# Two crossbar transposes put side by side, a gate before three loads, and one permute moved from GpSimd to VectorE

## The chip, the cores and the metric

The kernel runs on one NeuronCore of a Trainium2 chip. The metric is the time of one execution on the device in microseconds. Beside it there is a profile of one execution: the time of every instruction on TensorE (PE, with its weight loads as PEld), VectorE (DVE), ScalarE (ACT), GpSimd (POOL) and of the DMA issues of SyncE (SP), and of the DMA packets.

## The reference

Attention in two steps through 32 packed tokens, and behind it a feed-forward layer with the activation h·cos(h):

```python
def sm_attn(qq, kk, vv):
    s = scale * np.matmul(qq, kk.transpose(0, 1, 3, 2))
    s = s - np.max(s, axis=-1, keepdims=True)
    a = np.exp(s)
    a = a / (np.sum(a, axis=-1, keepdims=True) + 1e-09)
    return np.matmul(a, vv)
p_packed = sm_attn(p, k, v)              # p: (8, 8, 32, 64), k and v: (8, 8, 576, 64)
attn = sm_attn(q, p_packed, p_packed)    # q: (8, 8, 576, 64)
x = attn.transpose(0, 2, 1, 3).reshape(8 * 576, 512)
h = x @ w_in                             # (512, 2048)
out = (h * np.cos(h)) @ w_out            # (2048, 512)
```

All inputs and the output are float32; the kernel works in bfloat16 with float32 accumulation.

## The kernel before

The work goes through the eight batch elements, b = 0 to 7, one after the other. For each b the kernel loads q, k and v (`load`, L82: a DMA issued by GpSimd that also casts to bfloat16). k and q are needed with the head dimension on the partitions. For b = 0 and 1 and for k2 this is done by transposes on TensorE and copies (`pe_T`, L95); for q2, k3 and all later ones by a DMA transpose that SP issues (`xbar`, L91). v is needed in another order of its free dimension; `permute_v` (L86) copies it within SBUF, on GpSimd except for b = 0, which VectorE does.

`s1(b)` computes the scores of p against k and their exponentials on ScalarE, `a1_pe`, `a1_one` or `a1_xbar` transposes them, and `recips(b)` (L148) takes the reciprocals of the sums and multiplies them by the scale (the two small VectorE operations at L151 and L152). `pp(b)` multiplies by v and leaves the packed result, transposed, in `ppT`. `s2(b)` computes the scores of q against it, `sums2` and `normalise` their normalisation. Because the second attention's values are the same 32 packed rows for each head, `ppw(b, n)` multiplies them by w_in first (the tile `PPW`, in four pieces n of 512 columns), and `h_mm(b, fc)` (L248) multiplies PPW by the normalised weights `a2n` for one of 16 chunks fc of the hidden dimension. ScalarE takes the cosine of the result, VectorE multiplies it by h into `gT` (L263), and GpSimd copies a corner of gT into `joint` twice in each slot (L267). `out_gen` (L301) is the product with w_out, cut into small steps.

The order is written out by hand (`tc.manual_schedule()`); each engine executes its instructions in that order, and only semaphores between the engines delay them. The sixteen `h_mm` of one b are a slot (`slot`, L420). Between them stand steps of the previous b's output (`fill(n)`, n matmuls each), and hooks: a hook `(fc, f)` calls f behind `h_mm(s, fc)` and before the fills that follow it. Slot 0 is written out at L404. PSUM holds three buffers for `psA` (scores, `h_mm`, `pp`, transposes) and two banks for `ot` (output, and whatever asks for `bank()`).

p is loaded in three pieces into `p_raw`: rows for b = 0 and rows for b = 1 by SP at the start, the others by GpSimd at L387. `dup_p` (L340) casts them into `p_bf` twice, and `pack_p` (L112) transposes them on TensorE into `P2`, which `s1` reads.

Loads are issued by GpSimd in the order of the code, each one behind what stands before it on GpSimd. Where loads are to start only after a crossbar has finished, a *gate* is put before them: a copy of one element of the crossbar's result by GpSimd (`G.tensor_copy(out=gate, in_=xT["k", ...])`, L496 and L522). The buffers for q and v in bfloat16 are single (`bufs=1`), those for k double, `vp` has two, and `osb`, from which SP stores the output, has four.

`warm(n)` issues n matmuls on zeros that nothing reads.

Of the kernel before, what the change touches and what calls it, by code (L numbers as in the profile page):

```python
# [9 lines left out]
BF16 = mybir.dt.bfloat16  # L10
# [5 lines left out]
def kernel(  # L16
# [10 lines left out]
    nc = tc.nc  # L27
    B, H, S, D = q.shape
# [26 lines left out]
    V, ACT, G = nc.vector, nc.scalar, nc.gpsimd  # L55
# [5 lines left out]
    gate = const.tile([1, 1], BF16, name="gate")  # L61
    P2 = const.tile([128, B, H, NP], BF16, name="P2")
    p_raw = const.tile([128, 2 * B, D], FP32, name="p_raw")
# [4 lines left out]
    p_rows = p.rearrange("b h n d -> (b h n) d").rearrange("(g r) d -> r g d", r=128)  # L68
    srcs = {"k": k, "q": q, "v": v}
    bf, vp, xT, a1T, sums1, r1, rs1 = {}, {}, {}, {}, {}, {}, {}  # L70
    a2u, lns, a2n, PPW = {}, {}, {}, {}

    def copy(eng, out, in_):
        if eng is ACT:
            ACT.copy(out=out, in_=in_)  # L75
        else:
            eng.tensor_copy(out=out, in_=in_)  # L77

    def psa(dt=FP32):
        return A.tile([128, 2, 512 if dt == FP32 else 1024], dt, name="psA", tag="A")  # L80

    def load(n, b):  # L82
        bf[n, b] = bf_pool.tile([TP, H, C * D], BF16, name=n + "bf", tag=n + "bf", bufs=2 if n == "k" else 1)
        G.dma_start(out=bf[n, b], in_=srcs[n][b].rearrange("h (p c) d -> p h (c d)", c=C))  # L84

    def permute_v(b, eng=G):  # L86
        vp[b] = vp_pool.tile([TP, C, H * D], BF16, name="vp", tag="vp")
        copy(eng, vp[b].rearrange("p c (h d) -> p c h d", h=H),
             bf["v", b].rearrange("p h (c d) -> p c h d", c=C))

    def xbar(n, b):  # L91
        t = xT[n, b] = att_pool.tile([128, H * 3, TP], BF16, name=n + "T", tag=n + "T", bufs=2 if n == "k" else 1)
        nc.sync.dma_start_transpose(out=t, in_=bf[n, b].rearrange("p h x -> p (h x)"))

    def pe_T(n, b, engs=(V, V, V), groups=(0, 1, 2), own=False):  # L95
        if 0 in groups:
            xT[n, b] = att_pool.tile([128, H * 3, TP], BF16, name=n + "T", tag=n + "T", bufs=2 if n == "k" else 1)
        t = xT[n, b]
        flat = bf[n, b].rearrange("p h x -> p (h x)")
        for i in groups:  # L100
            ps = bank(BF16) if own else psa(BF16)[:, 0, :]
            for j in range(8):
                o = 8 * i + j
                nc.tensor.transpose(ps[:, j * TP:(j + 1) * TP], flat[:, o * 128:(o + 1) * 128],  # L104
                                    ident[0:TP, 0:TP])
            copy(engs[i], t[:, 8 * i:8 * i + 8].rearrange("p a x -> p (a x)"),
                 ps[:, 0:8 * TP])

    def bank(dt=FP32):
        return O.tile([128, 512 if dt == FP32 else 1024], dt, name="ot", tag="ot")  # L110

    def pack_p(b0, b1, flat=None):  # L112
        ng = 2 * (b1 - b0)
        if flat is None:
            flat = psa(BF16).rearrange("p a x -> p (a x)")
        for g in range(ng):
            nc.tensor.transpose(flat[:, g * 128:(g + 1) * 128],
                                p_bf[:, 2 * b0 + g].rearrange("p t d -> p (t d)"), ident)
        V.tensor_copy(out=P2[:, b0:b1].rearrange("p b h n -> p (b h n)"), in_=flat[:, 0:ng * 128])
# [14 lines left out]
    def s1(b, later=False):  # L134
        ps = scores(P2[:, b], xT["k", b])
        sm = sums1[b] = small.tile([128, 2], FP32, name="sums1")

        def exps():
            for y in range(2):
                ACT.activation(  # L140
                    out=a1[b % 2][:, y, :, 0:TP].rearrange("p (e m) x -> p e m x", e=2),
                    in_=ps[y][:, :, 0:HS].rearrange("p e (m x) -> p e m x", m=3),
                    func=AF.Exp, scale=scale, accum_out=sm[:, y:y + 1])
        if later:
            return exps
        exps()
# [22 lines left out]
    def a1_one(b):  # L169
        t = a1T[b] = att_pool.tile([128, 2, C, 128], BF16, name="a1T", tag="a1T")  # L170
        ps = psa(BF16)
        for y in range(2):
            for c in range(C):
                nc.tensor.transpose(ps[0:TP, y, c * 128:(c + 1) * 128], a1[b % 2][:, y, c, 0:TP], ident)
        for y in range(2):
            copy(V, t[0:TP, y].rearrange("p c x -> p (c x)"), ps[0:TP, y, 0:C * 128])

    def pp(b, own=False, engs=(V, ACT)):
        ps = bank() if own else psa()[:, 0, :]
        for hp in range(4):  # L180
            for j in range(C):
                c = 2 * (j % 3) + j // 3
                nc.tensor.matmul(ps[:, hp * 64:(hp + 1) * 64], vp[b][:, c, hp * 128:(hp + 1) * 128],  # L183
                                 a1T[b][0:TP, :, j, 32 * hp:32 * hp + 32], start=(j == 0), stop=(j == C - 1))
        pv = ps[:, 0:256].rearrange("p (a y x) -> p a y x", a=4, y=2)
        t = ppT[b % 2].rearrange("p (a y) x -> p a y x", y=2)
        for y in range(2):
            r = slice(64 * y, 64 * y + 64)
            copy(engs[0], t[r, :, y, :], pv[r, :, y, :])
        for y in range(2):  # L190
            r = slice(64 * y, 64 * y + 64)
            z = slice(64 - 64 * y, 128 - 64 * y)
            copy(engs[1], t[z, :, y, :], pv[r, :, y, :])
# [27 lines left out]
    def s2(b):  # L221
        a2u[b] = att_pool.tile([128, 2, S], BF16, name="a2u", tag="a2u")
        ps = scores(ppT[b % 2], xT["q", b])
        for y in range(2):
            ACT.activation(out=a2u[b][:, y].rearrange("p (e x) -> p e x", e=2),  # L225
                           in_=ps[y][:, :, 0:HS], func=AF.Exp, scale=rs1[b][:, y:y + 1])
# [109 lines left out]
    def load_w_out(n):  # L336
        G.dma_start(out=w_out_bf[:, n * 4:(n + 1) * 4, :],
                    in_=moe_w_out.rearrange("(a p) n -> p a n", p=128)[:, n * 4:(n + 1) * 4, :])

    def dup_p(a, b, eng):  # L340
        for t in range(2):
            eng.tensor_copy(out=p_bf[:, a:b, t, :], in_=p_raw[:, a:b, :])

    def warm(n):
        wps = bank()
        for _ in range(n):
            nc.tensor.matmul(wps, wz[:, 0:128], wz, start=True, stop=True)  # L347

    for a in (0, 2):
        nc.sync.dma_start(out=p_raw[:, a:a + 2, :], in_=p_rows[:, a:a + 2, :])  # L350
    load("k", 0)
    load("v", 0)
    make_identity(nc, ident)
# [15 lines left out]
    pack_p(0, 1)  # L369
    warm(9)  # L370
    pe_T("k", 0, (V, ACT, V))
    s1(0)
    dup_p(2, 4, V)
    pack_p(1, 2, bank(BF16))
    permute_v(0, V)
    load("v", 1)
    load_w_in(3)
# [7 lines left out]
    for n in range(4):  # L385
        load_w_out(n)
    G.dma_start(out=p_raw[:, 4:, :], in_=p_rows[:, 4:, :])  # L387
    s2(0)
    warm(3)
    sums2(0, 0)  # L390
    sums2(0, 1)
    pe_T("k", 1, (V, V, V))
# [2 lines left out]
    cut_ppw, rest_ppw = ppw(0, 0, V, own=True, later=True, cuts=((0, 256), (256, 512)))  # L395
    normalise(0)
    s1_mm()
    cut_ppw()
    a1_one(1)
    rest_ppw()  # L400
    load("k", 2)
    permute_v(1)
    load("v", 2)
# [16 lines left out]
    def slot(s, hooks, keep=0, heavy={}):  # L420
        left = filler[1] - keep
        out_eng[:] = (ACT,) if s > 1 else (V, ACT)
        weight = [1 + heavy.get(fc, 0) for fc in range(NFC)]
        for fc in range(NFC):
            h_mm(s, fc)()
            quota = (left * sum(weight[:fc + 1])) // sum(weight) - (left + keep - filler[1])
            first = quota
            while hooks and hooks[0][0] == fc:
                if first == quota and fc in heavy:
                    first = quota // 2  # L430
                    fill(first)
                hooks.pop(0)[1]()
            fill(quota - first if first != quota else quota)

    def pw2(b, n=0, eng=None):
        ppw(b, n, eng)
        ppw(b, n + 1, eng)

    def tk(n, b, i):
        return lambda: pe_T(n, b, (V, V, V), (i,))  # L440

    ACT.preload_act_table_set(EXP_SET)
    fill(4)
    s2(1)
# [4 lines left out]
    fill(5)  # L449
    sums2(1, 0)  # L450
    sums2(1, 1)
    xbar("q", 2)
    permute_v(2)
    load("v", 3)
    permute_v(3)
    load("q", 3)
    ppw(1, 1, V)
    normalise(1)
    ACT.preload_act_table_set(SIN_SET)
    fill(14)  # L460
    slot(1, [(3, lambda: pw2(1, 2, (ACT, V))), (5, tk("k", 2, 0)), (6, tk("k", 2, 1)),
             (7, tk("k", 2, 2)), (8, lambda: load("k", 4)), (9, lambda: pack_p(2, 5)),
             (11, lambda: pack_p(5, B)), (12, lambda: xbar("k", 3))], 4, {3: 3})

    ACT.preload_act_table_set(EXP_SET)
    out_eng[:] = V,
# [30 lines left out]
    for n, b in (("v", 4), ("q", 4), ("k", 5)):  # L497
        load(n, b)
    fill(5)
    slot(2, [(7, lambda: pp(3, engs=(ACT, ACT))), (11, lambda: pw2(3))], 5, {11: 3})  # L500

    for s in range(3, B):
        nxt = s + 1 < B
# [66 lines left out]
```

## Time and profile before

| what | value |
|---|---|
| time, median of 5 runs | 253.81 us |
| the five runs | 254.0, 253.81, 249.42, 254.47, 253.64 us |
| the profiled execution: its time | 254.0 us |
| its span, from the first to the last instruction | 252.2 us |
| busy PE, DVE, ACT, POOL | 235.4, 172.3, 167.0, 57.2 us |
| mean granted TensorE clock | 0.991 |
| bytes moved by DMA, mean rate | 37.09 MB, 147 GB/s |
| transposes by DMA: issues, us from issue to landing (median) | qT 6, 6.1; kT 5, 5.5; a1T 5, 3.9 |

How to read it: the times of the profile start at the first instruction, so the profiled execution's own time has 1.8 us around the span. An instruction row gives its start, its duration, the engine, the line of the kernel, and in brackets the idle time of its engine just before it and what ended it. The duration of a VectorE or GpSimd instruction contains the time that it waits for a port after it has started. A busy TensorE is not a TensorE at its peak: matmuls are pipelined, and their ends are modelled.

### The profile page before, as it was taken

The numbers are of one execution on the slowest core, as the hardware profiler recorded it, in microseconds if no ns is written. First come the engines' busy times: TensorE is split into PE (matmuls) and PEld (weight loads), VectorE is DVE, ScalarE is ACT, GpSimd is POOL, SyncE is SP. The second block draws the span as 40 slices with busy tenths as digits, with TensorE's granted clock in tenths as the row PEclk, the third lists the DMA queues.
The fourth block names the chain that finished last, engine by engine and source line by source line (L and its number), as shares of the span: only waits on it lengthen the run. The fifth ranks groups of instructions, "written<-read, shape, count | busy, mean of one in ns | idle before, by whom it ended". The sixth has DMA issues, their size and how long they took to land.

```text
span 252.2 us, 5036 instructions
## 1 busy us (share of the span) xinstructions
PE 235.4 (93%) x2004; PEld 132.4 (52%) x2038; DVE 172.3 (68%) x253; ACT 167.0 (66%) x278; POOL 57.2 (23%) x68
## 2 busy tenths in 40 slices
PE   8778599999999999999999999999999999999993
PEld 3454255556554565466545654565456554665452
DVE  2439998698877878577857666678767765876110
ACT  2358669865738588688867866888787784874000
POOL 8152622350070040404040405020500000000000
PEclk9999979999999999999999999999999999999999
DMA  6999999999979989998999992989291112202133
GB/s 98 202 206 205 205 207 228 198 175 92 200 137 198 203 167 206 169 215 150 222 191 205 160 231 56 171 171 212 72 181 42 42 44 55 72 10 66 48 86 83
DMA packets 63176, 37.09 MB, mean 147 GB/s; under 512 B 35793, under 2 KB 58577, under 8 KB 63153
## 3 DMA queue, kind: packets, MB, share of 16 engines
q0 software_dynamic: 23152, 18.75, 49.5%
q1 hardware_dynamic: 39840, 17.90, 36.8%
q8 instruction: 16, 0.26, 0.4%
q10 hardware_dynamic: 160, 0.13, 0.2%
q14 instruction: 8, 0.06, 0.1%
HBM read 37.22 MB, written 9.44 MB: 185 GB/s over the span
## 4 chain that ended last, share of the span: by engine, by line
PE 77%; DVE 10%; ACT 5%; DMA 4%; issue 3%; POOL 0%; DVEq 0%; ACTq 0%; POOLq 0%
PE ot L309 44%; PE psA L256 22%; DVE gT L263 4%; DMA vbf<-in_v_dram 4%; PE psA L207 3%; PE psA L129 2%; PE psA L183 2%; DVE rs L152 2%; ACT cosT L260 2%; PE ot L295 1%; DVE PPW L77 1%; PE psA L233 1%; ACT ppT L75 1%; DVE a1T L77 1%; DVE a2n L243 1%
## 5 line engine op out<-in xcount | busy, mean ns | idle before, releaser
L309 PE MATMUL ot<-w_out_bf,gT 128*128 128x512 bf16 x482 | 127.2, 379 | 2.1 <-issue 1.3
L263 DVE TENSOR_TENSOR gT<-psA,cosT 128x576 bf16<-128x576 f32 x128 | 93.9, 755 | 26.5 <-ACT cosT L260 25.7
L260 ACT ACTIVATE cosT<-psA 128x576 bf16<-128x576 f32 x128 | 82.5, 651 | 31.6 <-PE psA L256 26.8
L256 PE MATMUL psA<-a2n,PPW 128*128 128x288 bf16 x512 | 84.7, 289 | 4.8 <-DVE gT L263 3.4
L309 PEld LDWEIGHTS <-gT 128*128 128x128 bf16 x512 | 47.8, 98 | 42.9 <-issue 6.4
L256 PEld LDWEIGHTS <-PPW 128*128 128x128 bf16 x512 | 49.7, 98 | 38.5 <-issue 7.8
L77 DVE CAST PPW<-psA 128x1024 bf16<-128x1024 f32 (+1 forms) x23 | 26.9, 1175 | 11.8 <-PE psA L207 11.7
L267 POOL COPY joint<-gT 128x512 bf16<-128x512 bf16 x16 | 9.8, 614 | 91.3 <-DVE gT L263 91.3
L77 DVE COPY osb<-ot 128x512 f32<-128x512 f32 (+1 forms) x24 | 16.3, 678 | 17.0 <-PE ot L309 7.2
L77 POOL COPY vp<-vbf 96x3072 bf16<-96x3072 bf16 x7 | 19.2, 2748 | 19.6 <-DMA vbf<-in_v_dram 19.6
L243 DVE SCALAR_TENSOR_TENSOR a2n<-a2u,r,lns 128x576 bf16<-128x576 bf16 x16 | 12.7, 835 | 7.3 <-ACT lns L241 7.3
L75 ACT COPY osb<-ot 128x512 f32<-128x512 f32 (+1 forms) x13 | 7.3, 565 | 15.3 <-PE ot L309 10.6
L235 ACT ACTIVATE lns<-psA 128x576 f32<-128x576 f32 x16 | 10.1, 650 | 7.1 <-PE psA L233 6.5
L140 ACT ACTIVATE a<-psA 128x576 bf16<-128x576 f32 x16 | 10.2, 646 | 6.9 <-PE psA L129 6.9
L309 PE MATMUL ot<-w_out_bf,joint 128*128 128x512 bf16 x46 | 12.4, 379 | 0.1
L225 ACT ACTIVATE a2u<-psA,rs 128x576 bf16<-128x576 f32 x16 | 11.0, 737 | 1.0 <-PE psA L129 0.7
L75 ACT CAST ppT<-psA 64x128 bf16<-64x128 f32 x24 | 6.2, 259 | 7.5 <-DVE ppT L77 6.9
L207 PE MATMUL psA<-w_in_bf,ppT 64*32 64x512 bf16 x224 | 10.2, 381 | 0.0
L241 ACT ACTIVATE lns<-lns 128x576 f32<-128x576 f32 x16 | 10.0, 676 | 0.0
L347 PE MATMUL ot<-wz 128*128 128x512 bf16 x24 | 8.2, 477 | 1.4 <-DVE wz L359 1.2
L77 DVE COPY kT<-psA 128x768 bf16<-128x768 bf16 x8 | 4.2, 551 | 6.7 <-PE psA L104 6.5
L84 POOL DMA_DIRECT2D vbf<-in_v_dram x8 | 6.2, 774 | 7.2 <-DVE vp L77 5.2
(71 smaller groups left out, 156.2 us busy)
## 6 DMA issues: line engine op xcount, KB each, us to landing
kbf<-in_k_dram POOLq DMA_DIRECT2D x8, 576.0 KB, 12.2
vbf<-in_v_dram POOLq DMA_DIRECT2D x8, 576.0 KB, 8.1
qbf<-in_q_dram POOLq DMA_DIRECT2D x8, 576.0 KB, 10.1
out_dram<-osb SPq DMA_DIRECT2D x24, 192.0 KB, 2.7
out_dram<-osb SPq DMA_DIRECT2D x22, 128.0 KB, 2.4
w_in_bf<-in_moe_w_in_dram POOLq DMA_DIRECT2D x4, 512.0 KB, 16.5
w_out_bf<-in_moe_w_out_dram POOLq DMA_DIRECT2D x4, 512.0 KB, 20.5
out_dram<-osb SPq DMA_DIRECT2D x26, 64.0 KB, 2.1
```

What stands on the lines that cost most here:

```text
L75: ACT.copy(out=out, in_=in_)
L77: eng.tensor_copy(out=out, in_=in_)
L140: ACT.activation(out=a1[b % 2][:, y, :, 0:TP].rearrange("p (e m) x -> p e m x", e=2), in_=ps[y][:, :, 0:HS].rearrange("p e (m x) -> p e m ...
L207: nc.tensor.matmul(ps[y][32 * x:32 * x + 32, :], ppT[b % 2][r, 2 * x + y, :], w_in_bf[r, x, n * 512:(n + 1) * 512], start=True, stop=True)
L225: ACT.activation(out=a2u[b][:, y].rearrange("p (e x) -> p e x", e=2), in_=ps[y][:, :, 0:HS], func=AF.Exp, scale=rs1[b][:, y:y + 1])
L235: ACT.activation(out=lns[b][:, y].rearrange("p (e x) -> p e x", e=2), in_=ps[:, :, 0:HS], func=AF.Ln)
L241: ACT.activation(out=lns[b][:, y], in_=lns[b][:, y], func=AF.Exp, scale=-1.0)
L243: V.scalar_tensor_tensor(out=a2n[b][:, y], in0=a2u[b][:, y], scalar=r1[b][:, y:y + 1], in1=lns[b][:, y], op0=ALU.mult, op1=ALU.mult)
L256: nc.tensor.matmul(ps[:, e, 0:HS], PPW[b][:, y, fc * 128:(fc + 1) * 128], a2n[b][:, y, e * HS:(e + 1) * HS], start=(y == 0), stop=(y == 1))
L260: ACT.activation(out=csv, in_=ps[:, :, 0:HS], func=AF.Sin, bias=PI_HALF)
L263: V.tensor_tensor(out=gT[b][:, fc, :].rearrange("p (e x) -> p e x", e=2), in0=ps[:, :, 0:HS], in1=csv, op=ALU.mult)
L309: nc.tensor.matmul(pss[c], w, w_out_bf[:, fc, :], start=(fc == 0), stop=(fc == NFC - 1))
```

## The change

At the start, SP loads only the rows of p for b = 0; ScalarE issues the load of those for b = 1 behind its part of the first kT. The cast and the transposes of these rows move from behind `s1(0)` to before and behind `s2(0)`, with one warm matmul less. In front of slot 0, the second half of the first PPW piece is copied before `a1_one(1)` and not behind it.

In front of slot 1, `xbar("q", 2)`, the load of v3, `permute_v(3)` and the load of q3 go away, and the hooks with the load of k4 (fc 8) and `xbar("k", 3)` (fc 12) as well. Instead a hook at fc 4 issues both crossbars, and a hook at fc 12 issues, on GpSimd, a gate on the result of k3's crossbar and behind it the loads of q3, k4 and v3. In slot 2 a hook at fc 4 permutes v3 by VectorE.

```diff
--- before.py
+++ after.py
@@ -346,8 +346,7 @@
         for _ in range(n):
             nc.tensor.matmul(wps, wz[:, 0:128], wz, start=True, stop=True)
 
-    for a in (0, 2):
-        nc.sync.dma_start(out=p_raw[:, a:a + 2, :], in_=p_rows[:, a:a + 2, :])
+    nc.sync.dma_start(out=p_raw[:, 0:2, :], in_=p_rows[:, 0:2, :])
     load("k", 0)
     load("v", 0)
     make_identity(nc, ident)
@@ -369,9 +368,8 @@
     pack_p(0, 1)
     warm(9)
     pe_T("k", 0, (V, ACT, V))
+    ACT.dma_start(out=p_raw[:, 2:4, :], in_=p_rows[:, 2:4, :])
     s1(0)
-    dup_p(2, 4, V)
-    pack_p(1, 2, bank(BF16))
     permute_v(0, V)
     load("v", 1)
     load_w_in(3)
@@ -385,8 +383,10 @@
     for n in range(4):
         load_w_out(n)
     G.dma_start(out=p_raw[:, 4:, :], in_=p_rows[:, 4:, :])
+    dup_p(2, 4, V)
     s2(0)
-    warm(3)
+    pack_p(1, 2, bank(BF16))
+    warm(2)
     sums2(0, 0)
     sums2(0, 1)
     pe_T("k", 1, (V, V, V))
@@ -396,8 +396,8 @@
     normalise(0)
     s1_mm()
     cut_ppw()
+    rest_ppw()
     a1_one(1)
-    rest_ppw()
     load("k", 2)
     permute_v(1)
     load("v", 2)
@@ -439,6 +439,11 @@
     def tk(n, b, i):
         return lambda: pe_T(n, b, (V, V, V), (i,))
 
+    def next_loads():
+        G.tensor_copy(out=gate, in_=xT["k", 3][0:1, 0, 0:1])
+        for n, b in (("q", 3), ("k", 4), ("v", 3)):
+            load(n, b)
+
     ACT.preload_act_table_set(EXP_SET)
     fill(4)
     s2(1)
@@ -449,18 +454,14 @@
     fill(5)
     sums2(1, 0)
     sums2(1, 1)
-    xbar("q", 2)
     permute_v(2)
-    load("v", 3)
-    permute_v(3)
-    load("q", 3)
     ppw(1, 1, V)
     normalise(1)
     ACT.preload_act_table_set(SIN_SET)
     fill(14)
-    slot(1, [(3, lambda: pw2(1, 2, (ACT, V))), (5, tk("k", 2, 0)), (6, tk("k", 2, 1)),
-             (7, tk("k", 2, 2)), (8, lambda: load("k", 4)), (9, lambda: pack_p(2, 5)),
-             (11, lambda: pack_p(5, B)), (12, lambda: xbar("k", 3))], 4, {3: 3})
+    slot(1, [(3, lambda: pw2(1, 2, (ACT, V))), (4, lambda: (xbar("q", 2), xbar("k", 3))), (5, tk("k", 2, 0)), (6, tk("k", 2, 1)),
+             (7, tk("k", 2, 2)), (9, lambda: pack_p(2, 5)),
+             (11, lambda: pack_p(5, B)), (12, next_loads)], 4, {3: 3})
 
     ACT.preload_act_table_set(EXP_SET)
     out_eng[:] = V,
@@ -497,7 +498,7 @@
     for n, b in (("v", 4), ("q", 4), ("k", 5)):
         load(n, b)
     fill(5)
-    slot(2, [(7, lambda: pp(3, engs=(ACT, ACT))), (11, lambda: pw2(3))], 5, {11: 3})
+    slot(2, [(4, lambda: permute_v(3, V)), (7, lambda: pp(3, engs=(ACT, ACT))), (11, lambda: pw2(3))], 5, {11: 3})
 
     for s in range(3, B):
         nxt = s + 1 < B
```

## The prediction, made before the changed kernel was run

> **What bounds the kernel now.** I read the page first: the span, the busy times, and the chain that ended last by engine.
>
> ```profile
> span 252.2 us, 5036 instructions
> PE 235.4 (93%) x2004; PEld 132.4 (52%) x2038; DVE 172.3 (68%) x253; ACT 167.0 (66%) x278; POOL 57.2 (23%) x68
> ...
> PE 77%; DVE 10%; ACT 5%; DMA 4%; issue 3%; POOL 0%; DVEq 0%; ACTq 0%; POOLq 0%
> ```
>
> TensorE carries the end, so a microsecond counts only where TensorE stands still. Busy times by stretch say where that is (columns: stretch, its length, then busy us of PE, PEld, DVE, ACT, POOL, the granted clock, DMA share, GB/s).
>
> ```profile
> 28.20:32.00 3.80, 0.64 (x12) 0.37 (x5) 3.80 (x3) 1.42 (x3) 3.50 (x3) 1.00 1.29 203
> 32.00:41.00 9.00, 8.77 (x92) 5.71 (x93) 8.08 (x13) 6.92 (x14) 0.97 (x2) 0.81 1.25 207
> ...
> 84.00:100.00 16.00, 15.90 (x133) 9.99 (x134) 12.43 (x18) 13.52 (x24) 3.09 (x5) 1.00 1.08 186
> ```
>
> From 84 to 100 us TensorE idles 0.1 us in 16: nothing on SP, POOL or the DMA engines can gain there. The one large hole is 28.2 to 32.0, where PE works 0.64 of 3.80 us; after it the granted clock is 0.81 for 9 us. The timeline of that hole names its cause.
>
> ```profile
> 27.76 0.78 POOL L84 DMA_DIRECT2D kbf<-in_k_dram  x1 [1.83 <-DMA vbf<-in_v_dram]
> 27.96 3.36 DVE L152 TENSOR_SCALAR rs<-r 128x2 f32<-128x2 f32 x1
> 28.53 2.75 POOL L77 COPY vp<-vbf 96x3072 bf16<-96x3072 bf16 x1
> ...
> 32.03 0.28 PE L256 MATMUL psA<-a2n,PPW 128*128 128x288 bf16 x1 [3.20 <-DVE gT L263]
> ```
>
> A VectorE operation on two numbers (recips(1), L152) takes 3.36 us and ends with GpSimd's copy of v1 (28.53 + 2.75 = 31.28). Over all eight of them (minimum, median, maximum, ns) it is:
>
> ```profile
> L152 DVE TENSOR_SCALAR rs<-r x8: 168/170/3357, 13.2 to 184.1; 128x2 f32<-128x2 f32 x8
> ```
>
> So 3.2 us of it is waiting for GpSimd, and the multiply of gT behind it, which frees PSUM for TensorE, waits too. rs came 0.20 us after GpSimd began the DMA issue of k2. The runs shown are 249.42 once and 253.64 to 254.47 four times. I read that gap of 4.4 us as this race, won once: 3.2 us of idle PE plus a part of 9 x 0.19 = 1.7 us of lost clock. That is an inference; only a slow one was profiled.
>
> **The change part by part.** The sum is made against the profiled execution, 254.0 us (span 252.2 and 1.8 around it), 0.2 above the median of 253.81.
>
> 1. *p_raw 2:4 moves from SP to ACT behind the first kT copy.* One issue by ACT costs about 0.5 us (503 and 560 ns at L299), in an idle time of 0.49 us (9.99 to 10.47) before the first exponential. That may slip by 0.05 us, and behind it VectorE waits for v0 anyway (landed 11.21). The 64 KB leave the start, but q0, on which PE waits at 14.14, still has the same bytes ahead of it. SP has nothing behind it until 53.8. Value 0 (between -0.2 and +0.1).
>
> 2. *dup_p and pack_p of batch 1 move from 10.0 to behind the last qT copy, one warm matmul goes.* Work: two casts of 0.22 us, two PE transposes of 0.22 and a copy of 0.29. VectorE is idle from 16.46 to 19.05 and PE waits there for exponentials with warm matmuls, so the work by itself is hidden. Its place is the doubt, because GpSimd issues DMAs then:
>
> ```profile
> 2.17 0.77 POOL L84 DMA_DIRECT2D vbf<-in_v_dram  x1
> 2.78 0.46 DVE L342 CAST p_bf<-p_raw 128x128 bf16<-128x128 f32 x2 [0.54 <-DMA p_raw<-in_p_dram]
> ...
> 16.16 0.79 POOL L84 DMA_DIRECT2D qbf<-in_q_dram  x1 [2.12 <-PE psA L104]
> 16.94 1.51 POOL L337 DMA_DIRECT2D w_out_bf<-in_moe_w_out_dram  x2
> ```
>
> The same cast at 2.78, inside the issue of v0 (2.17 to 2.94), took its ordinary 0.23 us; by that row the new place costs nothing. rs at 27.96, 0.2 us into the issue of k2, was held through it. The Trainium skill (SBUF — State Buffer, section Who interferes with whom) says that VectorE, in a mode that uses two ports, and GpSimd take one port pair as an exclusive lock for a whole instruction, and its box on software descriptors counts the writing of DMA descriptors among GpSimd's uses. That speaks against this move: by the rule the casts, 0.30 us into the issue of q1, wait up to 18.45, pack_p's transposes hold PE in order, and sums2 slips from 17.64 to some 18.8 to 19.3. I take the middle: a coin toss between 0 and +1.2 us on the chain of VectorE that ends at rs.
>
> 3. *rest_ppw before a1_one(1).* Today VectorE stands 0.26 us before a1T (waiting for L174) and copies the rest of PPW behind it:
>
> ```profile
> 22.92 1.02 DVE L77 COPY a1T<-psA 96x768 bf16<-96x768 bf16 x2 [0.26 <-PE psA L174]
> 23.86 0.74 DVE L77 CAST PPW<-ot 128x256 bf16<-128x256 f32 x2
> ```
>
> The casts now fill that hole, and the banks for L207 (waiting at 24.33) are free some 0.4 us earlier, so ACT's copy of PPW and the cosines follow. The chain to rs gains about 0.27 us: rs at 27.69 against GpSimd's 27.76.
>
> 4. *What 2 and 3 make of the stall.* GpSimd's time is set by the landing of v1, which no edit moves. If the casts are held (half), rs comes at about 28.9, inside the copy, and is released at 31.3 as now: its end is fixed by GpSimd, so the delay is swallowed and nothing is lost. If they are not held, rs is 0.07 us ahead on paper. With one win in five from 0.20 behind, the spread is some 0.24 us; 0.27 better gives a win in 6 of 10. Together 0.5 x 0.6 = 0.3 for an escape, 0.7 for the same stall. An escape is worth 4.4 us (253.8 less 249.4).
>
> 5. *Slot 1: xbars of q2 and k3 behind the first four stores, one gate, then the loads.* Before:
>
> ```profile
> 53.77 4.89 SPq L93 DMA_TRANSPOSE qT<-qbf  x1
> 64.52 7.21 SPq L93 DMA_TRANSPOSE kT<-kbf  x1
> ...
> 70.65 2.74 POOL L77 COPY vp<-vbf 96x3072 bf16<-96x3072 bf16 x1 [15.95 <-DMA vbf<-in_v_dram]
> 71.50 1.91 DVE L152 TENSOR_SCALAR rs<-r 128x2 f32<-128x2 f32 x1
> ```
>
> q2 took up to 14.9 us to land beside the load of v3, undisturbed ones 5.4. Now: stores of 0.6 us each from 51.2, xbar q2 from about 54 to 55, landing about 63, k3 landing about 68. They are used at 73.8 (s2(2)) and 76.3 (s1(3)): both in time before, both in time now, value 0. Queued behind them on SP are stores of chunks 2 and 3 (4 osb buffers, no one waits). Behind the gate on GpSimd stand q3, k4, v3 and the last joint copy of slot 1, which TensorE reads at 94.9. The gate opens near 68; three issues of 0.77 us, and v3, behind 1.7 MB at 205 GB/s, lands near 80. q3 is there at 72 instead of 80; xbar q3 can then start near 76, k4's and the next loads some 2 us earlier. No one waited for them on TensorE: value 0.
>
> 6. *v3's copy leaves GpSimd.* rs(2) at 71.50 then takes 0.17 unless the three issues reach it; PE's wait for ppT and the s2(2) matmuls, 73.82 to 74.93 where the same sixteen take 0.44 at 42.52, shorten by about 0.4. Bounds 0 and -0.6.
>
> 7. *v3's copy enters VectorE in slot 2 behind gT of fc 4.* The same copy on VectorE took 0.956 us at 11.24. Around it:
>
> ```profile
> 87.29 2.98 DVE L263 TENSOR_TENSOR gT<-psA,cosT 128x576 bf16<-128x576 f32 x4 [0.27 <-ACT cosT L260]
> ...
> 89.62 0.86 PE L183 MATMUL psA<-a1T,vp 96*128 96x64 bf16 x24
> ```
>
> The four multiplies (fc 3 to 6) run without a gap. psA has three buffers, so pp(3) at 89.62 takes that of fc 5, whose multiply ended at 89.57; now it ends near 90.4. No fill stands between h_mm(7) and pp in PE's order, so PE stands about 0.8 us (bounds 0.2, if the slack of 0.05 were larger than it looks, and 1.0). TensorE has nowhere to get it back.
>
> Sum with the stall kept: 254.0 + 0.8 - 0.4 = 254.4; measured, less 0.2: **254.2**. With the escape: 254.2 - 4.4 = **249.8**.
>
> **Rivals.** *The race is won* (0.30): 249.8. For it: one run of before, and the margin of 0.07; against: the margin is smaller than the spread, and the casts may be held by GpSimd's issues. *v3 comes late* (0.08): VectorE executes in order, so if v3 has not landed at 88.7 the whole slot waits. It decides from a gate later than about 77.7 (11 us before 88.7), since v3 is now the third load behind it. If the xbars keep the 14.9 and 10.8 us that they had beside loads and run one after the other from 55, the gate is at 81 and v3 lands at 92: 3.3 us more, 257.5; with loads as slow as the slowest before (19.2), about 7 more, 261. Against it: after 58 only stores run beside the xbars. *The crossbars are not alone, and nothing moves* (within the forecast): q2's starts while k3 still loads; as TensorE waits for neither, the time is that of the forecast.
>
> **How the numbers follow.** Forecast, stall kept: 0.60, own range 253.2 to 255.4 (items 6 and 7 at their ends). Escape 0.30, late v3 0.08, other 0.02. The range 249.3 to 255.6 takes in the first two and leaves out about 0.15. Faster by over 2% means under 248.7: only an escape with items 6 and 7 both at their good ends, 0.06. Slower by over 2% means over 258.9: the worse half of late v3 and what I overlooked, 0.08. 2% is about what a measurement of this kernel can tell from no change.
>
> **What would show it.** Right: L152 with a maximum near 2 to 3 us ending with GpSimd's first vp copy; the casts of p_bf near 16.5 either 0.22 us or over 1; rs(2) at 0.17; pp(3) waiting some 0.8 us for gT in slot 2; both xbars landed before 70. Wrong: all eight L152 at 0.17 and PE full from 28 to 32 (the rival at 249.8), or a VectorE copy in slot 2 that waits for the DMA of v3.

## The result and the profile after

| | before | changed |
|---|---|---|
| median of the runs | 251.28 us (80 runs) | 249.95 us (43 runs) |
| lowest to highest | 248.78 to 255.64 | 249.69 to 251.47 |
| runs over 252 us | 36 of 80 | 0 of 43 |
| the profiled execution: time, span | 254.0, 252.2 us | 249.71, 247.9 us |

The runs of before that were known at the prediction were the first five of the 80. The ratios of two kernels, here and below, use only runs within 1.5% of the lowest of the same kernel, so they say little of the bad runs, for which the counts over 252 us stand; by them the two kernels are the same: ratio 0.9992, interval 0.998 to 1.0004. So the change makes the good runs no better. It takes away the bad ones, and brings the median down by 0.5%. The likeliest case of the prediction, 254.2, was wrong; what came is near the number of its first rival, 249.8.

The page of the changed kernel: span, busy times, and the chain that ended last by engine.

```profile
span 247.9 us, 5035 instructions
PE 233.8 (94%) x2003; PEld 131.6 (53%) x2037; DVE 168.0 (68%) x254; ACT 166.7 (67%) x278; POOL 54.8 (22%) x68
...
PE 73%; DMA 12%; DVE 7%; ACT 3%; issue 2%; POOL 2%; SPq 0%; DVEq 0%; POOLq 0%
```

TensorE does the same work in a shorter span. The busy times in the two stretches around the old hole (stretch, length, then PE, PEld, DVE, ACT, POOL, clock, DMA share, GB/s):

```profile
28.20:32.00 3.80, 2.41 (x23) 1.08 (x22) 3.29 (x6) 2.57 (x6) 3.53 (x2) 1.00 1.30 204
32.00:41.00 9.00, 8.89 (x116) 5.53 (x117) 7.08 (x10) 8.45 (x17) 3.48 (x5) 1.00 1.24 207
```

PE works 2.41 us where it worked 0.64, and the granted clock stays at 1.00 where it was 0.81. The eight operations of L152, and the timeline of the place where one of them stood 3.36 us:

```profile
L152 DVE TENSOR_SCALAR rs<-r x8: 168/169/319, 12.2 to 179.8; 128x2 f32<-128x2 f32 x8
```

```profile
26.71 0.17 DVE L152 TENSOR_SCALAR rs<-r 128x2 f32<-128x2 f32 x1
...
28.36 0.78 POOL L84 DMA_DIRECT2D kbf<-in_k_dram  x1 [2.28 <-DMA vbf<-in_v_dram]
...
29.13 2.76 POOL L77 COPY vp<-vbf 96x3072 bf16<-96x3072 bf16 x1
...
30.33 0.41 PE L207 MATMUL ot<-w_in_bf,ppT 64*32 64x512 bf16 x8 [1.05 <-DMA w_in_bf<-in_moe_w_in_dram]
```

rs now comes 1.65 us ahead of GpSimd's k2 issue; it came 0.20 us behind it. The last row is new: TensorE is so early that it waits 1.05 us for the fourth piece of w_in.

Where the 4.3 us between the two profiles lie is read from the places where ScalarE changes its table, which are the same points of both programs. The two around slot 0, before and then changed:

```profile
22.31 1.28 ACT L260 ACT_TABLE_LOAD   x1
...
42.01 1.28 ACT L442 ACT_TABLE_LOAD   x1
```

```profile
21.28 1.28 ACT L260 ACT_TABLE_LOAD   x1
...
37.73 1.28 ACT L447 ACT_TABLE_LOAD   x1
```

All of them (us; "slot 0" means the table load at the head of slot 0, and so on):

| from the table load to the next | before | changed | difference |
|---|---|---|---|
| start to slot 0 | 22.31 | 21.28 | -1.03 |
| slot 0 to s2(1) | 19.70 | 16.45 | -3.25 |
| s2(1) to slot 1, and slot 1 to s1(2) | 5.07, 20.34 | 5.06, 20.35 | 0 |
| s1(2) to slot 2 | 13.31 | 12.64 | -0.67 |
| slot 2 to s2(3) | 18.96 | 19.63 | +0.67 |
| s2(3) to the table load of slot 7 | 115.51 | 115.52 | 0 |

The start, in the changed kernel (first copy of kT; it began at 8.85 before), and the casts of p in their new place:

```profile
7.88 1.24 DVE L77 COPY kT<-psA 128x768 bf16<-128x768 bf16 x2 [2.98 <-PE psA L104]
...
15.13 0.80 POOL L84 DMA_DIRECT2D qbf<-in_q_dram  x1 [2.12 <-PE psA L104]
...
15.34 0.61 DVE L342 CAST p_bf<-p_raw 128x128 bf16<-128x128 f32 x2
...
15.91 1.51 POOL L337 DMA_DIRECT2D w_out_bf<-in_moe_w_out_dram  x2
```

The two casts take 0.61 us together and not 0.35 as at 10.0 us before, and end with the first of GpSimd's three issues, not with the last. Slots 1 and 2 (SP's two crossbars, the gate, rs(2), VectorE's copy of v3, pp(3)):

```profile
55.39 3.72 SPq L93 DMA_TRANSPOSE qT<-qbf  x1
59.16 2.96 SPq L93 DMA_TRANSPOSE kT<-kbf  x1
...
64.06 0.18 POOL L443 COPY gate<-kT 1x1 bf16<-1x1 bf16 x1 [8.11 <-DMA kT<-kbf]
...
67.23 0.32 DVE L152 TENSOR_SCALAR rs<-r 128x2 f32<-128x2 f32 x1
...
83.68 0.95 DVE L77 COPY vp<-vbf 96x3072 bf16<-96x3072 bf16 x1
...
84.55 2.08 DVE L263 TENSOR_TENSOR gT<-psA,cosT 128x576 bf16<-128x576 f32 x3
...
85.35 0.86 PE L183 MATMUL psA<-a1T,vp 96*128 96x64 bf16 x24 [0.58 <-DVE gT L263]
```

The crossbars of q2 and k3 land 5.2 and 4.8 us after their issue; before they took 14.9 and 10.8 (the same line of the views of the two tiles, before and then changed):

```profile
DMA to landing us min/median/max: 14.9/14.9/14.9
...
DMA to landing us min/median/max: 10.8/10.8/10.8
```

```profile
DMA to landing us min/median/max: 5.2/5.2/5.2
...
DMA to landing us min/median/max: 4.8/4.8/4.8
```

rs(2) costs 0.32 and not 1.91. pp(3) waits 0.58 us for gT, which the copy of v3 holds up.

### The profile page after: what moved, and what is told of

Its sections match the earlier page's. It is cut to its first block, busy times and chain, and to the rows that moved or that the text cites. A ratio compares the mean times of both kernels' runs of the same rounds, so it can differ in the third digit from the quotient of the medians.

```text
span 247.9 us, 5035 instructions
## 1 busy us (share of the span) xinstructions
PE 233.8 (94%) x2003; PEld 131.6 (53%) x2037; DVE 168.0 (68%) x254; ACT 166.7 (67%) x278; POOL 54.8 (22%) x68
## 4 chain that ended last, share of the span: by engine, by line
PE 73%; DMA 12%; DVE 7%; ACT 3%; issue 2%; POOL 2%; SPq 0%; DVEq 0%; POOLq 0%
PE ot L309 43%; PE psA L256 19%; DMA vbf<-in_v_dram 10%; DVE gT L263 4%; PE psA L207 3%; DMA out_dram<-osb 2%; PE psA L129 2%; PE psA L183 2%; ACT cosT L260 2%; PE ot L295 1%; PE psA L233 1%; POOL vp L77 1%; DVE PPW L77 1%; DVE vp L77 1%; ACT ppT L75 1%
## 5 line engine op out<-in xcount | busy, mean ns | idle before, releaser
L256 PE MATMUL psA<-a2n,PPW 128*128 128x288 bf16 x512 | 83.8, 286 | 1.9 <-DVE PPW L77 0.4
L77 POOL COPY vp<-vbf 96x3072 bf16<-96x3072 bf16 x6 | 16.5, 2750 | 3.9 <-DMA vbf<-in_v_dram 3.9
L183 PEld LDWEIGHTS <-vp 96*128 96x128 bf16 x192 | 6.6, 98 | 2.4 <-issue 1.1
```

Of the source, the lines that this page charges most:

```text
L256: nc.tensor.matmul(ps[:, e, 0:HS], PPW[b][:, y, fc * 128:(fc + 1) * 128], a2n[b][:, y, e * HS:(e + 1) * HS], start=(y == 0), stop=(y == 1))
```

## The experiments

A *lottery* is here a wait that comes in some runs of a program and not in others. Theory: before has two lotteries, and the change settles both. One is the port at 28 us (rs against GpSimd's copy of v1), the other is whether the crossbar of k3 lands before `s1(3)`. Rivals: only one of them counts; or the bad runs have a cause outside the kernel. The kernel before ran beside each group of kernels, on the same chip: beside e1 to e4 it had 31 of 68 runs over 252 us, beside e5, e6, e8 and e9 (on another chip) 2 of 11, beside e7 and e10 10 of 35. So a small number of bad runs says little in the second group. Of each kernel one run was profiled.

**One part of the change at a time.**

*The start alone* (e1_start), on the kernel before:

```diff
-    for a in (0, 2):
-        nc.sync.dma_start(out=p_raw[:, a:a + 2, :], in_=p_rows[:, a:a + 2, :])
+    nc.sync.dma_start(out=p_raw[:, 0:2, :], in_=p_rows[:, 0:2, :])
...
+    ACT.dma_start(out=p_raw[:, 2:4, :], in_=p_rows[:, 2:4, :])
     s1(0)
-    dup_p(2, 4, V)
-    pack_p(1, 2, bank(BF16))
...
+    dup_p(2, 4, V)
     s2(0)
-    warm(3)
+    pack_p(1, 2, bank(BF16))
+    warm(2)
```

> The kernel before with the start of the change alone: rows of p for b = 1 loaded by ScalarE behind the first kT, their casts and transposes moved behind the last qT copy. Theory (the start wins the race): k0 and v0 land about 1.0 us earlier (7.3 and 10.2 instead of 8.3 and 11.2), so rs at L152 comes near 27.0, ahead of GpSimd's k2 issue near 28; all eight L152 under 0.4 us, and the time sits at about 249.5 to 250 with a spread of under 1 us, as in the changed kernel. Rival (the 0.27 us of rest_ppw decide): the stall at L152 stays in at least half of the runs, and the median stays near 252 to 254.

Measured: median 252.59, 249.16 to 262.88; 12 of 22 runs over 252; ratio 1.0 (0.9967 to 1.0033). The mechanism came as the theory said and the time did not. In its profile, of a run at 251.17, all L152 are short and rs is 1.3 us ahead, but TensorE waits in a new place (L152, who waited for whom on PE, 60 to 98 us, and SP's row of that crossbar):

```profile
L152 DVE TENSOR_SCALAR rs<-r x8: 169/169/171, 12.3 to 181.3; 128x2 f32<-128x2 f32 x8
```

```profile
PE psA L129 <- DMA kT<-kbf: 1.8, 1, 1.8
```

```profile
62.10 7.73 SPq L93 DMA_TRANSPOSE kT<-kbf  x1
```

The program now wants k3 at 71.6 us, 4.7 earlier than in the profile of before, and k3's crossbar, which runs beside the load of v3 (landed at 68.5), lands only at 73.3. One lottery was won and the other lost. The runs of 253 to 255 us were not profiled, so a wait that costs so much more than 1.8 us is not shown, and the single run at 262.88 is not explained.

*rest_ppw alone* (e2_rest), on the kernel before:

```diff
+    rest_ppw()
     a1_one(1)
-    rest_ppw()
```

> The kernel before with rest_ppw in front of a1_one(1) and nothing else. Theory (the start wins the race): rs comes only about 0.27 us earlier, near 27.7, at the same time as the k2 issue; the runs stay spread from 249 to 254 as those of the kernel before, with somewhat more of them low. Rival (rest_ppw decides): all runs at 249 to 250, none above 252.

Measured: median 250.67, 249.24 to 253.9; 4 of 14 over 252; ratio 1.0007 (0.9971 to 1.0042). As the theory expected: the spread stays. From the first copy of kT to rs it is 18.89 us, against 19.11 before: the edit is worth 0.22 us there. This profile is of a run over 252 us, at 252.62, in which no L152 is held, so it shows the second lottery alone: TensorE waits for k3's crossbar, and then for that of a1, which stands behind on SP (who waited for whom on PE, 60 to 98 us):

```profile
PE psA L129 <- DMA kT<-kbf: 1.5, 1, 1.5
PE psA L183 <- DMA a1T<-a: 1.1, 1, 1.1
```

*Slots 1 and 2 alone* (e3_slot1): the changed kernel with the start and rest_ppw put back.

> The changed kernel with the start and the place of rest_ppw as before, so with the crossbars, the gate, the loads and v3's copy in slots 1 and 2 alone. Theory: the spread from 249 to 254 stays, since none of this comes before 28 us; from slot 0's end to slot 3's start the same time to within 0.2 us (0.7 gained before slot 2, 0.7 lost in it). Rival (the crossbars alone on the DMA engines are what makes the runs fast): all runs near 250.

Measured: 17 of 22 runs at 249.59 to 250.44, five at 254.11 to 255.18, nothing between; median 250.23, ratio 0.9998 (0.9982 to 1.0013). What this part takes away is everything in between, where 30 of the 68 runs of before lie. The profile is of one of the five, and shows the port (timeline):

```profile
28.00 0.78 POOL L84 DMA_DIRECT2D kbf<-in_k_dram  x1 [1.85 <-DMA vbf<-in_v_dram]
...
28.17 3.39 DVE L152 TENSOR_SCALAR rs<-r 128x2 f32<-128x2 f32 x1
...
28.77 2.75 POOL L77 COPY vp<-vbf 96x3072 bf16<-96x3072 bf16 x1
```

So the theory, by which the spread stays, was half wrong: this part removes one of the two lotteries. From slot 0's end to slot 3's start the profile has 58.02 us against 57.68 before, 0.14 more than the theory allowed.

**The port by itself.** *rs moved away from the copy* (e4_recips_early), on the kernel before:

```diff
-        if fc == 3:
+        if fc == 1:
             recips(1)
```

> The kernel before with recips(1) behind h_mm 1 of slot 0 and not behind h_mm 3; it is the same work some 1.3 us earlier on VectorE. Theory (the collision of L152 with GpSimd's copy is the whole of the spread): rs near 26.6, 0.17 us long, no hole on TensorE from 28 to 32; all runs between 248.5 and 251, none above 252, median near 250. Rival (the slow runs have another cause, a clock or the DMA rate): the spread to 254 stays.

Measured: 10 of 22 runs over 252, median 251.45, ratio 1.0047 (1.0018 to 1.0077). This is what the theory did not expect: the port is not the whole of the spread. In the profile, of a run at 251.09, L152 is never over 0.17 us and rs is 2.1 us ahead (L152, then who waited for whom on PE, 60 to 98 us):

```profile
L152 DVE TENSOR_SCALAR rs<-r x8: 169/170/171, 13.0 to 181.2; 128x2 f32<-128x2 f32 x8
```

```profile
PE psA L129 <- DMA kT<-kbf: 1.2, 1, 1.2
```

The 10 runs over 252, up to 256.13, were not profiled. That they lose by the same wait is inferred from what slots 1 and 2 take away.

*rs moved into the copy* (e5_recips_late), on the changed kernel:

```diff
-        if fc == 3:
+        if fc == 5:
             recips(1)
```

> The changed kernel with recips(1) behind h_mm 5 of slot 0 and not behind h_mm 3, so that rs (L152) comes near 28.8, behind GpSimd's issue of k2 (28.4). Theory (a lost race costs 3 to 4.5 us, in this kernel too): rs takes 2.5 to 3.3 us and ends with GpSimd's copy of v1, TensorE stands some 3 us between 29 and 32, and nearly all runs are at 253 to 254.5. Rival (the changed kernel is fast because the crossbars are out of the way, and has slack for this stall): all runs stay at 250 to 251.

Measured: median 253.79 (251.96 to 254.64, four runs), ratio 1.0138 (1.0085 to 1.0192) against before. The timeline of the lowest of them:

```profile
28.73 0.78 POOL L84 DMA_DIRECT2D kbf<-in_k_dram  x1 [1.87 <-DMA vbf<-in_v_dram]
...
29.50 2.75 POOL L77 COPY vp<-vbf 96x3072 bf16<-96x3072 bf16 x1
...
29.77 2.53 DVE L152 TENSOR_SCALAR rs<-r 128x2 f32<-128x2 f32 x1
...
33.00 1.19 PE L256 MATMUL psA<-a2n,PPW 128*128 128x288 bf16 x7 [1.56 <-DVE gT L263]
```

`recips(1)` two `h_mm` later, and the changed kernel has its median among the bad runs of before. TensorE stands 1.6 us in this run, not 3. A lost race costs 2.0 us here and up to 4.7 in the other three runs, whose granted clock was 0.986 to 0.992; the profiled one had 0.999.

**Both at once.** *Slots 1 and 2 as changed, rs early, start and rest_ppw as before* (e8_both_races): e3_slot1 with `fc == 1` for `recips(1)`.

> The kernel before with two edits: slots 1 and 2 as in the changed kernel, and recips(1) behind h_mm 1 of slot 0; the start and the place of rest_ppw stay as before. Theory (two lotteries, the port at 28 us and k3's crossbar before s1(3), make the whole spread): all runs between 249.3 and 251, as tight as the changed kernel, none above 252. Rival (the early start is needed as well): runs above 252 remain in at least a tenth.

Measured: 249.82 to 250.21 in five of six runs, 251.57 in one; median 250.19, ratio 1.001 (0.9973 to 1.0048). This is what the theory expected but for the one run, and it is weak evidence: beside it before had only 2 of 11 runs over 252, so six runs cannot exclude the rival. The profile says more. The kernel differs from e3_slot1 in the place of `recips(1)` alone, and slot 0 to s2(1) takes 15.56 us here, 19.22 in the profile of e3_slot1 with its stall. So the stall at L152 costs 3.66 us.

**What makes k3's crossbar late.** *v3 loaded beside the crossbars again* (e9_v3_beside), on the changed kernel:

```diff
     permute_v(2)
+    load("v", 3)
...
-        for n, b in (("q", 3), ("k", 4), ("v", 3)):
+        for n, b in (("q", 3), ("k", 4)):
```

> The changed kernel with the load of v3 issued as before, behind permute_v(2) near 54 us, so that it runs beside both crossbars; q3 and k4 stay behind the gate, VectorE still copies v3 in slot 2. Theory (the company of a load is what slows the crossbars): those of q2 and k3 take 8 to 12 us to land and not 5 to 6, k3 lands near 70 to 73 where s1(3) wants it near 71.3, and TensorE waits there in part of the runs: a spread of 1 to 4 us above 250. Rival (their early place in slot 1 is enough): time and spread as in the changed kernel, TensorE waits for no kT.

Measured: q2's crossbar lands after 10.4 us and not 5.2, k3's after 6.7 and not 4.8; median 250.96, 249.87 to 251.38, ratio 1.0028 (0.999 to 1.0066). So in this profile the company of a load slows q2's crossbar as expected; k3's, which was issued when v3 had just landed, is slowed less than expected. The place of the loss was not the one expected: k3 is in time, but the gate opens at 70.8 and not at 64.1, q3 comes later, and behind its crossbar on SP that of a1 is late for pp(3). SP's rows, then who waited for whom on PE:

```profile
55.70 8.33 SPq L93 DMA_TRANSPOSE qT<-qbf  x1
64.08 3.02 SPq L93 DMA_TRANSPOSE kT<-kbf  x1
```

```profile
PE psA L183 <- DMA a1T<-a: 2.0, 1, 2.0
```

**The start.** *p for b = 1 loaded by SP at the start again* (e7_p_early), on the changed kernel:

```diff
+    for a in (0, 2):
+        nc.sync.dma_start(out=p_raw[:, a:a + 2, :], in_=p_rows[:, a:a + 2, :])
-    nc.sync.dma_start(out=p_raw[:, 0:2, :], in_=p_rows[:, 0:2, :])
...
-    ACT.dma_start(out=p_raw[:, 2:4, :], in_=p_rows[:, 2:4, :])
```

> The changed kernel with the rows of p for b = 1 loaded by SP at the start, as before; their casts stay in the later place. Theory (those 64 KB hold up the first k): the first copy of kT starts at 8.5 to 9.2 and not at 7.9 to 8.35, rs (L152) comes near 27.3 with GpSimd's k2 issue near 28; time 0.2 to 0.6 us more, 250.2 to 250.5, with a lost race (over 252) in at most a few runs. Rival (the early k is chance, or comes from another edit): kT at 8 as in the changed kernel, and the same time.

Measured: kT at 8.45, rs at 27.26, k2 issue at 28.42; median 249.87, one run of 14 over 252 (255.13), ratio 0.9987 (0.9962 to 1.0013). Over all twelve profiles of this study the first copy of kT starts at 8.45 to 9.19 in the six with both loads at the start (mean 8.78) and at 7.88 to 8.35 in the six with one (mean 8.11). So the 64 KB hold up the first k by about 0.7 us. In the median nothing of it is left: against the changed kernel the profile has 0.55 us more before slot 0 and 0.49 less in it, where TensorE waits less for w_in (0.7 us here, 1.05 in the changed kernel).

**The price of v3 on VectorE, and a better version.** *v3 copied by GpSimd, in front of the gate of slot 2* (e6_v3_pool), on the changed kernel:

```diff
     a1_xbar(3)
     recips(3)
+    permute_v(3)
...
-    slot(2, [(4, lambda: permute_v(3, V)), (7, lambda: pp(3, engs=(ACT, ACT))), (11, lambda: pw2(3))], 5, {11: 3})
+    slot(2, [(7, lambda: pp(3, engs=(ACT, ACT))), (11, lambda: pw2(3))], 5, {11: 3})
```

> The changed kernel with v3 copied by GpSimd, in the idle time in front of the gate of slot 2 (behind recips(3) in the order of the code), and not by VectorE in slot 2. Theory (item 7 of the prediction): pp(3) does not wait for gT (0.6 us in the changed kernel); a2n of batch 2 may be held by GpSimd's copy for up to 0.4 us, hidden or not; time 0.3 to 0.7 us less, about 249.4. Rival (VectorE's copy is absorbed later in the slot): no difference, 249.9 to 250.0.

Measured: median 249.48, 249.17 to 249.58, ratio 0.9974 (0.994 to 1.0008). Slot 2 to s2(3) takes 18.96 us again, pp(3) waits for nothing. All six runs lie below the lowest of the changed kernel (249.69), though the two did not run side by side. GpSimd's row shows when v3 lands:

```profile
79.74 2.74 POOL L77 COPY vp<-vbf 96x3072 bf16<-96x3072 bf16 x1 [11.56 <-DMA vbf<-in_v_dram]
```

*That, and rs early* (e10_best): e6_v3_pool with `fc == 1` for `recips(1)`.

> The changed kernel with v3 copied by GpSimd in front of the gate of slot 2 and recips(1) behind h_mm 1 of slot 0. Theory: the gain of the first (0.5 us) stays and the race at L152 is won by over 1 us in every run; 249.3 to 249.7, no run above 250.5. Rival (recips(1) earlier delays gT on the path): 0.2 to 0.5 us more, 249.8 and over.

Measured: median 249.26, 22 runs from 249.1 to 249.59, ratio 0.9961 (0.9941 to 0.998) against before, which had 10 of 35 runs over 252 beside it. So with both lotteries settled no bad run is left. It is faster than before by 0.4%; its runs too lie below the lowest of the changed kernel, but the two did not run side by side, and what `recips(1)` adds to e6_v3_pool is not shown.

## Why the prediction was wrong, point by point

- **The reading of the five runs, and with it the odds of item 4**, is the step that failed. It took 249.42 against 253.64 to 254.47 as one race, lost four times in five, and from that came the spread of 0.24 us, the chance of 0.3 for an escape and the forecast with the stall kept. In e3_slot1, which has the start, the casts and rest_ppw of before, this race is lost in 5 runs of 22: the stall was the rarer case before any gain of items 1 to 3 is counted. The other bad runs have another cause: in e4_recips_early, whose profile has no stall at L152, 10 of 22 runs are over 252, and the run profiled in e2_rest, at 252.62, has no stall there and waits 2.6 us for crossbars. The profiled execution of before showed only the first lottery, because its stall made the program so late that k3's crossbar (landed at 75.3) was in time for `s1(3)` at 76.3.
- **Item 1 (p on ScalarE)**: valued at 0. It moves the first k by 0.7 us, 0.97 in the two profiles. At the end it is worth nothing that e7_p_early could measure, so the sum was not hurt, but the race was decided on paper by 0.07 us, and this term of 0.7 to 1.0 was left out of it. How much it moves the odds is not shown: without it 1 run of 14 is over 252 (e7_p_early), with it none of 43.
- **Item 2 (casts beside GpSimd's issues)**: a coin toss between 0 and 1.2 us. The first cast, 0.21 us into the issue, took 0.216 us; the second, 0.34 us into it, took 0.477 and ended with the issue. All seven profiles with the casts in this place have the same two times to 0.003 us. The loss is 0.26 us and hidden: sums2 still starts when its exponential is ready. The bound from the Trainium skill's rule of a lock for the whole instruction (SBUF — State Buffer, Who interferes with whom), taken over all three issues, was too high here; the row at 2.78 was nearer, though only the first of its two casts took 0.23 us, and the second took 0.32.
- **Item 3 (rest_ppw)**: 0.27 predicted, 0.22 measured in e2_rest.
- **Item 4 (the rest of it)**: rs was 1.65 us ahead in the profile, and no run of 43 went over 252 us. GpSimd's side moves more than was allowed for: k2's issue stood between 27.76 and 28.73 in twelve profiles, against the spread of 0.24. What an escape is worth was near: 4.4 predicted, 4.3 between the profiles. The parts do not agree so well. The stall alone costs 3.66 us (e8_both_races), and 1.0 of the 4.3 comes from the start, which item 1 put at 0; that 249.8 was met within 0.15 us is in part luck.
- **Item 5 (crossbars alone)**: valued at 0, since both landed in time in the one profile. In the kernel before that holds for a run with the stall, and not for one without it. k3's crossbar had 1.0 us of slack in a profile that was 4 us late, and without the stall TensorE waits 1.2 to 1.8 us for it (e1, e2, e4). The prediction priced an escape and did not ask whether k3 is in time then. The landing times came out earlier than predicted: about 63 and 68 predicted, 60.6 and 64.0 measured.
- **Item 6 (rs(2) free)**: 0.4 predicted, with 0.6 as the most; 0.67 measured in s1(2) to slot 2.
- **Item 7 (v3 on VectorE)**: 0.8 predicted, 0.67 measured, by the mechanism named (pp(3) waits 0.58 us for the multiply of fc 5); e6_v3_pool gives it back.
- **The rival of a late v3** did not come. v3 lands at 79.2, 13.1 us after its issue at 66.12 and 4.5 us ahead of its copy. That 80 was predicted is luck: the gate opened 4 us earlier than predicted (64.06, not 68), and from gate to landing it took 15 us and not 12.

## What to carry to other kernels

When the runs of a kernel spread and the profile shows one stall, look for the wait that this stall covers before pricing its removal: take away the stall alone (one line moved is enough) and see whether the spread goes. Where two engines race, compare the margin with how much either side moves from run to run: here 0.22 us from rest_ppw stood against 0.97 us by which k2's issue moved between profiles. A crossbar transpose that is needed soon should not share the DMA engines with a load that is not: q2's landed after 10.4 us beside the load of v3, and after 5.2 without it.

## What the hardware showed that was not expected

- A VectorE operation on 128 x 2 numbers that started 0.17 to 0.20 us into a GpSimd DMA issue, over 0.5 us ahead of the copy behind that issue, was held to the end of the copy (before and e3_slot1: 3.36 and 3.39 us). The multiplies of gT, which read PSUM, were not held beside the same copy: three of them took 0.75 us each at 28.7 to 30.8 in the changed kernel, whose copy ran from 29.13 to 31.89. A cast that started 0.21 us into an issue with another DMA behind it was not held at all. What decides between the two is open.
- The DMA transpose of q2 landed after 5.2 to 5.8 us in six profiles in which only the end of the load of k3 ran beside it, and after 7.4 in e3_slot1, where that load ended later. Beside the load of v3 (576 KB) it took 10.4 us in e9_v3_beside, and 11.8 to 14.9 in the four kernels with slot 1 as before. That of k3 landed after 4.8 to 5.0 us with no load beside it.
- 64 KB of p in packets of 256 bytes delayed the first load by 0.7 us; at the 157 GB/s that the DMA engines moved from 2 to 8 us before, the bytes alone would be some 0.4 us, by estimate.
- In the twelve profiles a late first k (8.8 to 9.2) goes with an early k2 issue (27.8 to 28.1), an earlier one (7.9 to 8.7) with 28.4 to 28.7, which makes the race at L152 more uneven than either alone. Why was not tried.
